# Decode attention and SwiGLU on one core: the negation of the row maximum moved from GpSimd to ScalarE, a fourth V buffer, and a feed-forward computed transposed

## The chip, the core and the metric

The kernel runs on one core of a Trainium2 chip. A core has five engines with an instruction stream each: TensorE (PE in the profile; PEld are its weight loads), VectorE (DVE), ScalarE (ACT), GpSimd (POOL) and SyncE (SP), which here only starts transfers. They meet at semaphores. Sixteen DMA engines move data from the memory of the chip (HBM) to the on-chip memory of 128 partitions (SBUF); TensorE writes to PSUM. The metric is the time of one execution in microseconds on the device, the median of several.

## The reference

One decode step for a batch of 4: layer norm, attention over a cache of 4096 positions with 32 heads of width 192, a residual, layer norm, a SwiGLU feed-forward, a residual. All inputs are bf16.

```python
q = (layernorm(x) @ wq)                    # 4 x 640 @ 640 x 6144 -> 4 x 32 heads x 192
scores = einsum("bhqd,bhkd->bhqk", q, k_cache) * 192 ** -0.5     # k_cache 4 x 32 x 4096 x 192
o = einsum("bhqk,bhkd->bhqd", softmax(scores), v_cache)
h = x + o.reshape(4, 1, 6144) @ wo
n = layernorm(h)
out = h + (silu(n @ w_gate) * (n @ w_up)) @ w_down               # w_gate, w_up 640 x 1536
```

There is no reuse: each of the 128 pairs of head and batch row (called heads below, n = 4 x head + row) has its own K and V of 1.57 MB each.

## The kernel before, in words

**A head.** K of one head lies on 128 partitions with 32 rows of 192 each (`kbuf`, 4 buffers), V likewise (`vbuf`, `NB_V` = 3 buffers). Its query is spread over all partitions by a small TensorE product (`qbmm`, L679) and copied by ScalarE (`qbcopy`, L518, into `qb`). VectorE forms the 4096 scores in 32 multiply-and-sum instructions (L422), which write one column of `S` each, and takes the maximum per partition (L431, `pmax`). GpSimd takes the maximum over partitions (L336, `gmax`) and negates it (L339, `negmax`). ScalarE computes exp(S + negmax) into `E` with the sum per partition (L585, `rowsum`). GpSimd sums over partitions (L343, `gsum`). VectorE takes the reciprocal (L437) and scales `E` (L447). TensorE then adds up the head's output in 32 products (`pv`, L694). GpSimd's loop has these three operations in this order for each head and nothing else.

**Heads by TensorE.** Every eighth head, n = 5, 13, ... 117 (15 of them, `p_heads`), gets its scores from TensorE instead: `pwork` transposes K in eight slabs of 8 transposes (L737, L739), ScalarE copies each slab out of PSUM (`pcopies`, L542 and L543), and TensorE multiplies it with the query in 8 one-column products (L751, L753). ScalarE copies the scores to `S` (L556). Such a head takes its place in the softmax four heads later (the list `order`; the rank of a head is its place there).

**The order of the work** is written out by hand for each engine. VectorE's step s does the scores of head s, the maximum of rank s-1, the reciprocal of rank s-2 and the scaling of rank s-3. ScalarE's step s does the exponential of rank s, then the slab copies of head s+1 if that is a p head, then the query copy of head s+4, then copies of outputs. TensorE's step s does the query products of head s+4 (and of head s+5 where the step has a `pwork`), `pwork` of head s+2 if that is a p head, and `pv` of rank s-2; the output projection of a pair of heads comes a few steps later (`ott`, `womm`). SyncE issues the loads in one order: K of head m as soon as head m-4 is used up (for a p head: transposed), then V of rank m-5 as soon as `pv` of NB_V ranks earlier is done. A load that has to wait holds up those behind it.

**Ends.** Ahead of the loop stands a layer norm (with 1/sqrt as exp(-0.5 ln), L561 and L564). After it come the residual (L452), the second layer norm (L621, L624), the transposes of its result into `hlnT` (L815), and the feed-forward in three chunks of 512 columns: five gate and five up products of 512 columns each with `hlnT` as weights (L824, L827), then three copies out of PSUM by ScalarE (L633 sigmoid, L635, L637), before the next chunk. VectorE multiplies the three results (L472, L475), TensorE transposes the product in 12 pieces (L834), ScalarE copies it (L642), and the down product follows (L839, L841).

Of the kernel before, what the change touches and what calls it, by code (L numbers as in the profile page):

```python
# [5 lines left out]
ACT = mybir.ActivationFunctionType  # L6
ALU = mybir.AluOpType
AX = mybir.AxisListType
ReduceOp = bass.bass_isa.ReduceOp
BF16 = mybir.dt.bfloat16  # L10
# [15 lines left out]
def bass_sequential_preLN__gqa_block_cached__swiglu_ffn__decode_kernel(  # L26
# [12 lines left out]
    B, _sq, D = A_x.shape  # L39
# [3 lines left out]
    F = B_w_gate.shape[1]  # L43
# [5 lines left out]
    KT = D // 128  # L49
    FT = F // 128  # L50
    NQBLK = QD // 512
    NFC = F // 512
# [3 lines left out]
    PAIRK = (2 * DH) // 128  # L56
    assert PAIRK * 128 == 2 * DH
    WOK = QD // 128
    NB_K, NB_V, NQB, NS, NP = 4, 3, 4, 4, 4
    NE = 2 * B  # L60
    QLA = 4
    att_scale = float(DH) ** -0.5
# [3 lines left out]
    def hb(n):  # L66
        return n // B, n % B
# [3 lines left out]
    NPH = len(p_heads)  # L71
# [10 lines left out]
    NSLAB = JQ // SLAB_T  # L82
# [29 lines left out]
    for k in range(NH):  # L112
        n = order[k]
        s = e4slot(n)
# [58 lines left out]
    stp = [pe_step_chunk[j] for j in sorted(pe_step_chunk)]  # L173
    assert all(stp[i + 1] > stp[i] + 3 for i in range(len(stp) - 1)), stp

    DV_VEPS1, DV_XLN = 4, 5
    DV_H, DV_VEPS2, DV_HLN, DV_GU, DV_FINAL = 6, 9, 10, 12, 13
    AC_RSTD1, AC_XLNT = 2, 3
    AC_RSTD2, AC_HLNT = 5, 6
    AC_GUC = [6 + 3 * (c + 1) for c in range(NFC)]  # L180
    AC_GU = AC_GUC[-1]
    AC_GUT = AC_GU + 1
    PE_XT = 1
    PE_HT = 2
    PE_FFN1 = [2 + (c + 1) for c in range(NFC)]
    PE_GUT = PE_FFN1[-1] + 1
    PE_DOWN = PE_GUT + 1
    PL_READY = 2 + NE

    es = ExitStack()  # L190
    with es:  # L191
        E_ = es.enter_context
# [4 lines left out]
        rstd1 = E_(nc.sbuf_tensor("rstd1", [B, 1], FP32))  # L197
# [13 lines left out]
        gmax = E_(nc.sbuf_tensor("gmax", [128, NP], FP32))  # L211
        negmax = E_(nc.sbuf_tensor("negmax", [128, NP], FP32))
# [8 lines left out]
        wg_sb = E_(nc.sbuf_tensor("wg_sb", [128, KT, F], BF16))  # L221
        wu_sb = E_(nc.sbuf_tensor("wu_sb", [128, KT, F], BF16))
# [4 lines left out]
        rstd2 = E_(nc.sbuf_tensor("rstd2", [B, 1], FP32))  # L227
        hln_bf = E_(nc.sbuf_tensor("hln_bf", [B, D], BF16))
        hlnT = E_(nc.sbuf_tensor("hlnT", [128, KT, B], BF16))
        sig_sb = E_(nc.sbuf_tensor("sig_sb", [B, F], BF16))  # L230
        g_sb = E_(nc.sbuf_tensor("g_sb", [B, F], BF16))
        u_sb = E_(nc.sbuf_tensor("u_sb", [B, F], BF16))
        gu_sb = E_(nc.sbuf_tensor("gu_sb", [B, F], BF16))
        guT = E_(nc.sbuf_tensor("guT", [128, FT, B], BF16))
        out_bf = E_(nc.sbuf_tensor("out_bf", [B, D], BF16))
        psqb = [E_(nc.psum_tensor(f"psqb{i}", [128, 512], FP32)) for i in range(2)]
# [5 lines left out]
        psT32 = psT.bitcast(FP32)  # L242
        psM16 = psM.bitcast(BF16)
        PSS_COL0 = 0
        QCOL_A = DH
        QCOL_B = DH + 1
        OTC0 = 512
# [70 lines left out]
        @block.gpsimd  # L318
        def _(eng):
            eng.memset(ident[:, :], 0.0)  # L320
            i1 = eng.memset(sel[:, :, :], 0.0)
            c_pl.inc(i1)
            for s in range(NE):
                i1 = eng.memset(E4[s][:, :, :], 0.0)
                c_pl.inc(i1)
            eng.wait_ge(c_pl.sem, 1)
            eng.affine_select(out=ident[:, :], in_=ident[:, :], compare_op=ALU.not_equal,
                              fill=1.0, base=0, pattern=[[-1, 128]], channel_multiplier=1)
            i1 = eng.affine_select(out=sel[:, :, :], in_=sel[:, :, :], compare_op=ALU.not_equal,
                                   fill=1.0, base=0, pattern=[[-1, B], [0, 128]], channel_multiplier=1)  # L330
            pl_ready = c_pl.inc(i1)
            assert pl_ready == PL_READY
            for k in range(NH):
                s = k % NP
                eng.wait_ge(c_rm.sem, k + 1)
                i1 = eng.partition_all_reduce(gmax[:, s:s + 1], pmax[:, s:s + 1], 128, ReduceOp.max)  # L336
                c_ar.inc(i1)
                eng.wait_ge(c_ar.sem, k + 1)
                i1 = eng.tensor_scalar(out=negmax[:, s:s + 1], in0=gmax[:, s:s + 1],  # L339
                                       scalar1=-1.0, scalar2=None, op0=ALU.mult)  # L340
                c_neg.inc(i1)
                eng.wait_ge(c_exp.sem, k + 1)
                i1 = eng.partition_all_reduce(gsum[:, s:s + 1], rowsum[:, s:s + 1], 128, ReduceOp.add)  # L343
                c_tot.inc(i1)
# [43 lines left out]
        def _(eng):  # L388
# [11 lines left out]
            i1 = eng.tensor_scalar(out=rstd1[:, :], in0=mv1[:, 1:2], scalar1=1e-5, scalar2=None, op0=ALU.add)  # L400
            v = c_dv.inc(i1)
            assert v == DV_VEPS1
            eng.wait_ge(c_ac.sem, AC_RSTD1)
            i1 = eng.tensor_scalar(out=xln_bf[:, :], in0=x_f[:, :], scalar1=mv1[:, 0:1], scalar2=rstd1[:, 0:1],
                                   op0=ALU.subtract, op1=ALU.mult)
            v = c_dv.inc(i1)
# [56 lines left out]
            i1 = eng.tensor_scalar(out=rstd2[:, :], in0=mv2[:, 1:2], scalar1=1e-5, scalar2=None, op0=ALU.add)  # L463
            v = c_dv.inc(i1)
            assert v == DV_VEPS2
            eng.wait_ge(c_ac.sem, AC_RSTD2)
            i1 = eng.tensor_scalar(out=hln_bf[:, :], in0=h_f[:, :], scalar1=mv2[:, 0:1], scalar2=rstd2[:, 0:1],
                                   op0=ALU.subtract, op1=ALU.mult)
            v = c_dv.inc(i1)
            assert v == DV_HLN  # L470
            eng.wait_ge(c_ac.sem, AC_GU)
            i1 = eng.tensor_tensor(out=gu_sb[:, :], in0=g_sb[:, :], in1=sig_sb[:, :], op=ALU.mult)  # L472
            v = c_dv.inc(i1)
            eng.wait_ge(c_dv.sem, v)
            i1 = eng.tensor_tensor(out=gu_sb[:, :], in0=gu_sb[:, :], in1=u_sb[:, :], op=ALU.mult)  # L475
            v = c_dv.inc(i1)
            assert v == DV_GU
            eng.wait_ge(c_pe.sem, PE_DOWN)
# [5 lines left out]
        def _(eng):  # L484
# [73 lines left out]
                assert v2 == pi + 1  # L558

            eng.wait_ge(c_dv.sem, DV_VEPS1)  # L560
            i1 = eng.activation(out=rstd1[:, :], in_=rstd1[:, :], func=ACT.Ln)  # L561
            v = c_ac.inc(i1)
            eng.wait_ge(c_ac.sem, v)
            i1 = eng.activation(out=rstd1[:, :], in_=rstd1[:, :], func=ACT.Exp, scale=-0.5)  # L564
            v = c_ac.inc(i1)
            assert v == AC_RSTD1
            eng.wait_ge(c_pe.sem, PE_XT)
            i1 = eng.activation(out=xlnT[:, :, :], in_=psT[:, 0:KT * B], func=ACT.Copy)
            v = c_ac.inc(i1)
# [6 lines left out]
            for s in range(NH + 8):  # L576
                k = s
                if k < NH:
                    m = order[k]
                    hm, bm = hb(m)  # L580
                    eng.wait_ge(c_neg.sem, k + 1)
                    prv = prev_same_slot[m]
                    if prv is not None:
                        eng.wait_ge(c_pv.sem, rank[prv] + 1)
                    i1 = eng.activation(out=E4[e4slot(m)][:, :, bm], in_=S[k % NS][:, :], func=ACT.Exp,  # L585
                                        bias=negmax[:, (k % NP):(k % NP) + 1], scale=1.0,
                                        accum_out=rowsum[:, (k % NP):(k % NP) + 1])
                    v2 = c_exp.inc(i1)
                    assert v2 == k + 1
# [28 lines left out]
            assert c_oc.n == NGRP and c_otc.n == NPAIR and c_qbc.n == NH and c_exp.n == NH and c_qc.n == NQBLK  # L618
            assert c_kc.n == NPH * NSLAB and c_pS.n == NPH
            eng.wait_ge(c_dv.sem, DV_VEPS2)  # L620
            i1 = eng.activation(out=rstd2[:, :], in_=rstd2[:, :], func=ACT.Ln)  # L621
            v = c_ac.inc(i1)
            eng.wait_ge(c_ac.sem, v)
            i1 = eng.activation(out=rstd2[:, :], in_=rstd2[:, :], func=ACT.Exp, scale=-0.5)  # L624
            v = c_ac.inc(i1)
            assert v == AC_RSTD2
            eng.wait_ge(c_pe.sem, PE_HT)
            i1 = eng.activation(out=hlnT[:, :, :], in_=psT[:, 0:KT * B], func=ACT.Copy)
            v = c_ac.inc(i1)
            assert v == AC_HLNT  # L630
            for c in range(NFC):
                eng.wait_ge(c_pe.sem, PE_FFN1[c])
                i1 = eng.activation(out=sig_sb[:, c * 512:(c + 1) * 512], in_=psqb[0][0:B, 0:512], func=ACT.Sigmoid)  # L633
                c_ac.inc(i1)
                i1 = eng.activation(out=g_sb[:, c * 512:(c + 1) * 512], in_=psqb[0][0:B, 0:512], func=ACT.Copy)  # L635
                c_ac.inc(i1)
                i1 = eng.activation(out=u_sb[:, c * 512:(c + 1) * 512], in_=psqb[1][0:B, 0:512], func=ACT.Copy)  # L637
                v = c_ac.inc(i1)
                assert v == AC_GUC[c]
            assert v == AC_GU  # L640
            eng.wait_ge(c_pe.sem, PE_GUT)
            i1 = eng.activation(out=guT[:, :, :], in_=psT[:, 0:FT * B], func=ACT.Copy)  # L642
            v = c_ac.inc(i1)
            assert v == AC_GUT

        @block.tensor
        def _(eng):
# [169 lines left out]
            assert v == PE_HT  # L817
            eng.wait_ge(c_ac.sem, AC_HLNT)
            eng.wait_ge(sem_ffn, 48)
            for c in range(NFC):  # L820
                if c >= 1:
                    eng.wait_ge(c_ac.sem, AC_GUC[c - 1])
                for k in range(KT):
                    eng.matmul(psqb[0][0:B, 0:512], lhsT=hlnT[:, k, :], rhs=wg_sb[:, k, c * 512:(c + 1) * 512],  # L824
                               start=(k == 0), stop=(k == KT - 1))
                for k in range(KT):
                    i1 = eng.matmul(psqb[1][0:B, 0:512], lhsT=hlnT[:, k, :], rhs=wu_sb[:, k, c * 512:(c + 1) * 512],  # L827
                                    start=(k == 0), stop=(k == KT - 1))
                v = c_pe.inc(i1)
                assert v == PE_FFN1[c]  # L830
            eng.wait_ge(c_dv.sem, DV_GU)
            eng.wait_ge(c_ac.sem, AC_GU)
            for k in range(FT):
                i1 = eng.transpose(out=psT[:, k * B:(k + 1) * B], in_=gu_sb[0:B, k:F:FT], identity=identB)  # L834
            v = c_pe.inc(i1)
            assert v == PE_GUT
            eng.wait_ge(c_ac.sem, AC_GUT)
            for k in range(FT):
                eng.matmul(acc[0:B, 0:512], lhsT=guT[:, k, :], rhs=wd_sb[:, k, 0:512],  # L839
                           start=(k == 0), stop=(k == FT - 1))  # L840
# [34 lines left out]
```

## Time and profile before

| | |
|---|---|
| median of 6 executions | 2244.94 us (2239.03 to 2255.18) |
| profiled execution | span 2237.2 us, 23426 instructions |
| busy: PE, PEld, DVE, ACT, POOL | 935.1, 667.7, 1080.1, 235.3, 136.8 us |
| moved by DMA | 425.80 MB, mean 190 GB/s |
| mean granted TensorE clock | 0.619 |

A row of the groups gives line, engine, operation, output and inputs, the number of instructions, the busy time in us, the mean of one in ns, and after the bar the idle time of the engine just ahead of them with what ended most of it. "issue" stands where the trace shows nothing that the engine waited for. Engine names with a q (POOLq) are the sequencer of that engine. In the timeline a row gives start, length, engine, line, operation, and in brackets the idle time ahead of it.

### The profile page before, as it was taken

To read this page: it belongs to the slowest core of one execution; us is meant where nothing else is said; L and a number is where in the kernel's file an instruction comes from. 1 tells how busy PE (TensorE), PEld (TensorE's weight loads), DVE (VectorE), ACT (ScalarE), POOL (GpSimd) and SP (SyncE) were. 2 spreads that over 40 slices of the span, in tenths; PEclk is the share of its full clock that TensorE was granted. 3 is DMA by queue.
4 is the path that set the end of the run, shared out by engine and by line. 5 is a ranking of instruction groups with operands and counts; after the bars stand their busy time and mean duration, and the time that the engine had idled before them with its cause. 6 is when DMAs were issued, how large, how long until landed. Compare 5 with 4: busy or idle time off the path is not lost.

```text
span 2237.2 us, 23426 instructions
## 1 busy us (share of the span) xinstructions
PE 935.1 (42%) x6439; PEld 667.7 (30%) x6439; DVE 1080.1 (48%) x7631; ACT 235.3 (11%) x735; POOL 136.8 (6%) x400
## 2 busy tenths in 40 slices
PE   1162532635326262352634425453262634426235
PEld 0141321424214242241422314332141422314222
DVE  5465444555535555444554536555354554545551
ACT  1010100201001010110101002010010101001001
POOL 0000000000000000000000000000000000000000
PEclk7565565665656666566655656656565665656667
DMA  7354383542737436274361745527374361736430
GB/s 288 122 214 185 117 342 122 242 188 109 293 148 281 171 120 272 101 317 173 154 246 68 305 176 209 225 74 292 122 281 182 153 250 71 310 144 249 183 113 1
DMA packets 44339, 425.80 MB, mean 190 GB/s; under 512 B 4520, under 2 KB 5808, under 8 KB 11056
## 3 DMA queue, kind: packets, MB, share of 16 engines
q1 hardware_dynamic: 38192, 404.65, 45.8%
q10 hardware_dynamic: 6016, 19.66, 2.5%
q8 instruction: 51, 0.84, 0.1%
q14 instruction: 80, 0.66, 0.1%
HBM read 424.29 MB, written 0.01 MB: 190 GB/s over the span
## 4 chain that ended last, share of the span: by engine, by line
issue 77%; PE 13%; POOL 5%; ACT 3%; DVE 1%; POOLq 1%; ACTq 0%; DVEq 0%
PE psqb L739 4%; PE psqb L737 4%; POOL gsum L343 2%; PE psT L751 2%; PE psT L753 2%; POOL gmax L336 2%; POOL negmax L339 1%; ACT E L585 1%; DVE kbuf L422 1%; ACT kt L543 1%; ACT kt L542 0%; PE psO L694 0%; POOLq L339 0%; POOLq L191 0%; PE psqb L824 0%
## 5 line engine op out<-in xcount | busy, mean ns | idle before, releaser
L422 DVE CUSTOM_DVE_ANT_0 kbuf<-kbuf,qb 128x192 bf16<-128x192 bf16 x3616 | 1019.2, 353 | 13.5 <-ACT qb L518 13.3
L694 PE MATMUL psO<-vbuf,E 128*4 128x192 bf16 x4096 | 518.6, 307 | 387.7 <-DVE E L447 371.1
L694 PEld LDWEIGHTS psO<-vbuf,E 128*4 128x4 bf16 x4096 | 422.6, 106 | 470.3 <-DVE E L447 380.6
L437 DVE RECIPROCAL rtot<-gsum 128x1 f32<-128x1 f32 x128 | 21.0, 164 | 1101.3 <-POOL gsum L343 1101.3
L422 DVE DVE_READ_ACCUMULATOR2_ANT S<- 128x1 f32 x3616 | 295.6, 82 | 0.0
L679 PE MATMUL psM<-QO_sb,sel 4*128 4x192 bf16 x113 | 32.7, 290 | 626.8 <-ACT qb L518 319.2
L585 ACT ACTIVATE E<-S,negmax 128x32 bf16<-128x32 f32 x128 | 46.7, 365 | 1627.9 <-POOL negmax L339 1627.8
L679 PEld LDWEIGHTS psM<-QO_sb,sel 4*128 4x128 bf16 x113 | 10.7, 95 | 651.5 <-issue 414.6
L751 PE MATMUL psT<-qcolA,kt 128*128 128x1 bf16 x480 | 88.6, 185 | 183.9 <-ACT kt L543 183.9
L739 PE MATMUL psqb<-ident,kbuf 128*64 128x128 bf16 x480 | 151.7, 316 | 0.0
L737 PE MATMUL psqb<-ident,kbuf 128*128 128x128 bf16 x480 | 138.1, 288 | 0.0
L343 POOL PARTITION_ALL_REDUCE gsum<-rowsum x128 | 51.3, 401 | 981.6 <-issue 888.8
L751 PEld LDWEIGHTS psT<-qcolA,kt 128*128 128x128 bf16 x480 | 49.6, 103 | 203.1 <-issue 171.2
L339 POOL TENSOR_SCALAR negmax<-gmax 128x1 f32<-128x1 f32 x128 | 36.6, 286 | 1044.5 <-issue 1044.5
L542 ACT ACTIVATE kt<-psqb 128x512 bf16<-128x512 bf16 x120 | 71.1, 592 | 160.6 <-PE psqb L739 160.6
L753 PE MATMUL psT<-qcolB,kt 64*128 64x1 bf16 x480 | 87.8, 183 | 0.0
L739 PEld LDWEIGHTS psqb<-ident,kbuf 128*64 128x64 bf16 x480 | 61.4, 128 | 56.1
L543 ACT ACTIVATE kt<-psqb 64x512 bf16<-64x512 bf16 x120 | 69.4, 579 | 0.0
L737 PEld LDWEIGHTS psqb<-ident,kbuf 128*128 128x128 bf16 x480 | 49.8, 104 | 48.1 <-issue 2.7
L336 POOL PARTITION_ALL_REDUCE gmax<-pmax x128 | 56.3, 440 | 22.7 <-DVE pmax L431 22.7
L518 ACT ACTIVATE qb<-psM 128x192 bf16<-128x192 f32 x113 | 36.2, 320 | 157.0 <-PE psM L679 157.0
L753 PEld LDWEIGHTS psT<-qcolB,kt 64*128 64x128 bf16 x480 | 48.9, 102 | 7.0
(74 smaller groups left out, 232.9 us busy)
## 6 DMA issues: line engine op xcount, KB each, us to landing
kbuf<-in_A_k_cache_dram SPq DMA_DIRECT2D x128, 1536.0 KB, 8.6
vbuf<-in_A_v_cache_dram SPq DMA_DIRECT2D x128, 1536.0 KB, 10.1
wo_sb<-in_A_wo_dram ACTq DMA_DIRECT2D x16, 480.0 KB, 3.5
wq_sb<-in_A_wq_dram ACTq DMA_DIRECT2D x4, 1280.0 KB, 5.9
wg_sb<-in_B_w_gate_dram ACTq DMA_DIRECT2D x1, 1920.0 KB, 13.1
wu_sb<-in_B_w_up_dram ACTq DMA_DIRECT2D x1, 1920.0 KB, 13.4
wd_sb<-in_B_w_down_dram ACTq DMA_DIRECT2D x1, 1920.0 KB, 14.1
wq_sb<-in_A_wq_dram SPq DMA_DIRECT2D x1, 1280.0 KB, 5.8
```

Source lines behind the costliest of these rows:

```text
L336: i1 = eng.partition_all_reduce(gmax[:, s:s + 1], pmax[:, s:s + 1], 128, ReduceOp.max)
L339: i1 = eng.tensor_scalar(out=negmax[:, s:s + 1], in0=gmax[:, s:s + 1], scalar1=-1.0, scalar2=None, op0=ALU.mult)
L343: i1 = eng.partition_all_reduce(gsum[:, s:s + 1], rowsum[:, s:s + 1], 128, ReduceOp.add)
L422: i1 = eng.tensor_tensor_reduce(out=sl, in0=sl, in1=qb[qs][:, :], scale=1.0, scalar=0.0, op0=ALU.mult, op1=ALU.add, accum_out=S[ss][:, j:j ...
L542: eng.activation(out=kt1[g % 2][:, :], in_=psb16[g % 2][:, 0:SW], func=ACT.Copy)
L543: i1 = eng.activation(out=kt2[g % 2][:, :], in_=psb16[g % 2][0:64, SW:2 * SW], func=ACT.Copy)
L585: i1 = eng.activation(out=E4[e4slot(m)][:, :, bm], in_=S[k % NS][:, :], func=ACT.Exp, bias=negmax[:, (k % NP):(k % NP) + 1], scale=1.0, ac ...
L694: i1 = eng.matmul(psO[h % 2][0:B, 0:DH], lhsT=E4[e4slot(m)][:, j, :], rhs=vbuf[k % NB_V][:, j * DH:(j + 1) * DH], start=(first and j == 0) ...
L737: eng.transpose(out=psb16[g % 2][:, i * 128:(i + 1) * 128], in_=kbuf[sk][:, j * DH:j * DH + 128], identity=ident[:, :])
L739: i1 = eng.transpose(out=psb16[g % 2][0:64, SW + i * 128:SW + (i + 1) * 128], in_=kbuf[sk][:, j * DH + 128:j * DH + DH], identity=ident[:, :])
L751: eng.matmul(psT32[:, PSS_COL0 + j:PSS_COL0 + j + 1], lhsT=kt1[g % 2][:, i * 128:(i + 1) * 128], rhs=qcolA[qs][:, 0:1], start=True, stop=F ...
L753: i1 = eng.matmul(psT32[:, PSS_COL0 + j:PSS_COL0 + j + 1], lhsT=kt2[g % 2][0:64, i * 128:(i + 1) * 128], rhs=qcolB[qs][0:64, 0:1], start=F ...
```

## The change

It has four parts. The negation of the maximum goes from GpSimd to ScalarE, directly ahead of the exponential that uses it. V gets a fourth buffer. Both layer norms use Sqrt on ScalarE and a reciprocal on VectorE instead of Ln and Exp on ScalarE. The feed-forward is computed transposed: slices of the gate and up weights (128 columns, every twelfth) are TensorE's stationary operand and `hlnT` (4 columns) is the moving one, 60 products for gate and 60 for up, so that the results stand as 128 x 48 in PSUM and need no copies and no transposes ahead of the down product. The aim is less work on GpSimd and ScalarE's PSUM copies, more slack for V, and a shorter end.

```diff
-    NB_K, NB_V, NQB, NS, NP = 4, 3, 4, 4, 4
+    NB_K, NB_V, NQB, NS, NP = 4, 4, 4, 4, 4
...
# GpSimd, in the loop over heads
                 i1 = eng.partition_all_reduce(gmax[:, s:s + 1], pmax[:, s:s + 1], 128, ReduceOp.max)
                 c_ar.inc(i1)
-                eng.wait_ge(c_ar.sem, k + 1)
-                i1 = eng.tensor_scalar(out=negmax[:, s:s + 1], in0=gmax[:, s:s + 1],
-                                       scalar1=-1.0, scalar2=None, op0=ALU.mult)
-                c_neg.inc(i1)
                 eng.wait_ge(c_exp.sem, k + 1)
...
# ScalarE, in the loop over steps
+                    eng.wait_ge(c_ar.sem, k + 1)
+                    i1 = eng.activation(out=negmax[:, (k % NP):(k % NP) + 1], in_=gmax[:, (k % NP):(k % NP) + 1],
+                                        func=ACT.Copy, scale=-1.0)
+                    c_neg.inc(i1)
                     eng.wait_ge(c_neg.sem, k + 1)
...
# layer norms (the second likewise): ScalarE, then VectorE
-            i1 = eng.activation(out=rstd1[:, :], in_=rstd1[:, :], func=ACT.Ln)
...
-            i1 = eng.activation(out=rstd1[:, :], in_=rstd1[:, :], func=ACT.Exp, scale=-0.5)
+            i1 = eng.activation(out=rstd1[:, :], in_=rstd1[:, :], func=ACT.Sqrt)
...
+            i1 = eng.reciprocal(rstd1[:, :], rstd1[:, :])
...
# feed-forward, TensorE (up likewise into psU)
-                for k in range(KT):
-                    eng.matmul(psqb[0][0:B, 0:512], lhsT=hlnT[:, k, :], rhs=wg_sb[:, k, c * 512:(c + 1) * 512],
-                               start=(k == 0), stop=(k == KT - 1))
+            for t in range(FT):
                 for k in range(KT):
+                    i1 = eng.matmul(psG[:, t * B:(t + 1) * B], lhsT=wg_sb[:, k, t:F:FT], rhs=hlnT[:, k, :],
+                                    start=(k == 0), stop=(k == KT - 1))
...
-                i1 = eng.transpose(out=psT[:, k * B:(k + 1) * B], in_=gu_sb[0:B, k:F:FT], identity=identB)
...
# feed-forward, ScalarE and VectorE
-                i1 = eng.activation(out=sig_sb[:, c * 512:(c + 1) * 512], in_=psqb[0][0:B, 0:512], func=ACT.Sigmoid)
-                i1 = eng.activation(out=g_sb[:, c * 512:(c + 1) * 512], in_=psqb[0][0:B, 0:512], func=ACT.Copy)
-                i1 = eng.activation(out=u_sb[:, c * 512:(c + 1) * 512], in_=psqb[1][0:B, 0:512], func=ACT.Copy)
+            i1 = eng.activation(out=sigT[:, :], in_=psG, func=ACT.Sigmoid)
...
+            i1 = eng.tensor_tensor(out=gsT[:, :], in0=psG, in1=sigT[:, :], op=ALU.mult)
...
+            i1 = eng.tensor_tensor(out=guT[:, :, :], in0=gsT[:, :], in1=psU, op=ALU.mult)
```

More of the change, by code (lines that the diff above doesn't have):

```diff
@@ L174, in bass_sequential_preLN__gqa_block_cached__swiglu_ffn__decode_kernel @@
     assert all(stp[i + 1] > stp[i] + 3 for i in range(len(stp) - 1)), stp
[L176 to L187, printed above, removed]
+    DV_VEPS1, DV_RSTD1, DV_XLN = 4, 5, 6
+    DV_H, DV_VEPS2, DV_RSTD2, DV_HLN, DV_GU, DV_FINAL = 7, 10, 11, 12, 14, 15
+    AC_SQRT1, AC_XLNT = 1, 2
+    AC_SQRT2, AC_HLNT, AC_SIG = 3, 4, 5
+    PE_XT, PE_HT, PE_FFN_G, PE_FFN_U, PE_DOWN = 1, 2, 3, 4, 5
     PL_READY = 2 + NE
@@ L229, in bass_sequential_preLN__gqa_block_cached__swiglu_ffn__decode_kernel @@
         hlnT = E_(nc.sbuf_tensor("hlnT", [128, KT, B], BF16))
[L230 to L233, printed above, removed]
+        sigT = E_(nc.sbuf_tensor("sigT", [128, FT * B], BF16))
+        gsT = E_(nc.sbuf_tensor("gsT", [128, FT * B], BF16))
         guT = E_(nc.sbuf_tensor("guT", [128, FT, B], BF16))
@@ L244, in bass_sequential_preLN__gqa_block_cached__swiglu_ffn__decode_kernel @@
         PSS_COL0 = 0
+        psG = psqb[0][:, 0:FT * B]
+        psU = psqb[1][:, 0:FT * B]
         QCOL_A = DH
@@ L402, in _ @@
             assert v == DV_VEPS1
-            eng.wait_ge(c_ac.sem, AC_RSTD1)
+            eng.wait_ge(c_ac.sem, AC_SQRT1)
+            i1 = eng.reciprocal(rstd1[:, :], rstd1[:, :])
+            v = c_dv.inc(i1)
+            assert v == DV_RSTD1
+            eng.wait_ge(c_dv.sem, v)
             i1 = eng.tensor_scalar(out=xln_bf[:, :], in0=x_f[:, :], scalar1=mv1[:, 0:1], scalar2=rstd1[:, 0:1],
@@ L465, in _ @@
             assert v == DV_VEPS2
-            eng.wait_ge(c_ac.sem, AC_RSTD2)
+            eng.wait_ge(c_ac.sem, AC_SQRT2)
+            i1 = eng.reciprocal(rstd2[:, :], rstd2[:, :])
+            v = c_dv.inc(i1)
+            assert v == DV_RSTD2
+            eng.wait_ge(c_dv.sem, v)
             i1 = eng.tensor_scalar(out=hln_bf[:, :], in0=h_f[:, :], scalar1=mv2[:, 0:1], scalar2=rstd2[:, 0:1],
@@ L470, in _ @@
             assert v == DV_HLN
-            eng.wait_ge(c_ac.sem, AC_GU)
-            i1 = eng.tensor_tensor(out=gu_sb[:, :], in0=g_sb[:, :], in1=sig_sb[:, :], op=ALU.mult)
+            eng.wait_ge(c_ac.sem, AC_SIG)
+            i1 = eng.tensor_tensor(out=gsT[:, :], in0=psG, in1=sigT[:, :], op=ALU.mult)
             v = c_dv.inc(i1)
             eng.wait_ge(c_dv.sem, v)
-            i1 = eng.tensor_tensor(out=gu_sb[:, :], in0=gu_sb[:, :], in1=u_sb[:, :], op=ALU.mult)
+            eng.wait_ge(c_pe.sem, PE_FFN_U)
+            i1 = eng.tensor_tensor(out=guT[:, :, :], in0=gsT[:, :], in1=psU, op=ALU.mult)
             v = c_dv.inc(i1)
@@ L560, in _ @@
             eng.wait_ge(c_dv.sem, DV_VEPS1)
-            i1 = eng.activation(out=rstd1[:, :], in_=rstd1[:, :], func=ACT.Ln)
+            i1 = eng.activation(out=rstd1[:, :], in_=rstd1[:, :], func=ACT.Sqrt)
             v = c_ac.inc(i1)
-            eng.wait_ge(c_ac.sem, v)
-            i1 = eng.activation(out=rstd1[:, :], in_=rstd1[:, :], func=ACT.Exp, scale=-0.5)
-            v = c_ac.inc(i1)
-            assert v == AC_RSTD1
+            assert v == AC_SQRT1
             eng.wait_ge(c_pe.sem, PE_XT)
@@ L620, in _ @@
             eng.wait_ge(c_dv.sem, DV_VEPS2)
-            i1 = eng.activation(out=rstd2[:, :], in_=rstd2[:, :], func=ACT.Ln)
+            i1 = eng.activation(out=rstd2[:, :], in_=rstd2[:, :], func=ACT.Sqrt)
             v = c_ac.inc(i1)
[L623 to L626, printed above, removed]
+            assert v == AC_SQRT2
             eng.wait_ge(c_pe.sem, PE_HT)
@@ L630, in _ @@
             assert v == AC_HLNT
-            for c in range(NFC):
-                eng.wait_ge(c_pe.sem, PE_FFN1[c])
-                i1 = eng.activation(out=sig_sb[:, c * 512:(c + 1) * 512], in_=psqb[0][0:B, 0:512], func=ACT.Sigmoid)
-                c_ac.inc(i1)
-                i1 = eng.activation(out=g_sb[:, c * 512:(c + 1) * 512], in_=psqb[0][0:B, 0:512], func=ACT.Copy)
-                c_ac.inc(i1)
-                i1 = eng.activation(out=u_sb[:, c * 512:(c + 1) * 512], in_=psqb[1][0:B, 0:512], func=ACT.Copy)
[L638 to L642, printed above, removed]
+            eng.wait_ge(c_pe.sem, PE_FFN_G)
+            i1 = eng.activation(out=sigT[:, :], in_=psG, func=ACT.Sigmoid)
             v = c_ac.inc(i1)
-            assert v == AC_GUT
+            assert v == AC_SIG
         @block.tensor
@@ L819, in _ @@
             eng.wait_ge(sem_ffn, 48)
-            for c in range(NFC):
-                if c >= 1:
-                    eng.wait_ge(c_ac.sem, AC_GUC[c - 1])
+            if NPH > 0:
+                eng.wait_ge(c_kc.sem, NPH * NSLAB)
+            eng.wait_ge(c_qc.sem, NQBLK)
+            for t in range(FT):
                 for k in range(KT):
-                    eng.matmul(psqb[0][0:B, 0:512], lhsT=hlnT[:, k, :], rhs=wg_sb[:, k, c * 512:(c + 1) * 512],
-                               start=(k == 0), stop=(k == KT - 1))
+                    i1 = eng.matmul(psG[:, t * B:(t + 1) * B], lhsT=wg_sb[:, k, t:F:FT], rhs=hlnT[:, k, :],
+                                    start=(k == 0), stop=(k == KT - 1))
+            v = c_pe.inc(i1)
+            assert v == PE_FFN_G
+            for t in range(FT):
                 for k in range(KT):
-                    i1 = eng.matmul(psqb[1][0:B, 0:512], lhsT=hlnT[:, k, :], rhs=wu_sb[:, k, c * 512:(c + 1) * 512],
+                    i1 = eng.matmul(psU[:, t * B:(t + 1) * B], lhsT=wu_sb[:, k, t:F:FT], rhs=hlnT[:, k, :],
                                     start=(k == 0), stop=(k == KT - 1))
-                v = c_pe.inc(i1)
-                assert v == PE_FFN1[c]
+            v = c_pe.inc(i1)
+            assert v == PE_FFN_U
             eng.wait_ge(c_dv.sem, DV_GU)
-            eng.wait_ge(c_ac.sem, AC_GU)
-            for k in range(FT):
-                i1 = eng.transpose(out=psT[:, k * B:(k + 1) * B], in_=gu_sb[0:B, k:F:FT], identity=identB)
-            v = c_pe.inc(i1)
-            assert v == PE_GUT
-            eng.wait_ge(c_ac.sem, AC_GUT)
             for k in range(FT):
```

## The prediction

> **What bounds the kernel now.** I read the page's engine shares first (DVE 48%, PE 42%, DMA about half: nothing full), then its chain (77% "issue": an engine held by nothing the trace names), then the groups, to see which engine that is.
>
> ```profile
> L422 DVE CUSTOM_DVE_ANT_0 kbuf<-kbuf,qb 128x192 bf16<-128x192 bf16 x3616 | 1019.2, 353 | 13.5 <-ACT qb L518 13.3
> ...
> L343 POOL PARTITION_ALL_REDUCE gsum<-rowsum x128 | 51.3, 401 | 981.6 <-issue 888.8
> ...
> L339 POOL TENSOR_SCALAR negmax<-gmax 128x1 f32<-128x1 f32 x128 | 36.6, 286 | 1044.5 <-issue 1044.5
> ...
> L336 POOL PARTITION_ALL_REDUCE gmax<-pmax x128 | 56.3, 440 | 22.7 <-DVE pmax L431 22.7
> ```
>
> After the bar stands the idle time before a group. GpSimd is busy 137 us, yet idle 1044.5 us before its negation and 981.6 us before its sum: 2026 us of 2237. The order in time for GpSimd (start, length, line, idle before):
>
> ```profile
> 1002.43 0.40 POOL L343 PARTITION_ALL_REDUCE gsum<-rowsum  x1 [13.35 <-issue]
> 1002.75 0.44 POOL L336 PARTITION_ALL_REDUCE gmax<-pmax  x1
> 1010.53 0.31 POOL L339 TENSOR_SCALAR negmax<-gmax 128x1 f32<-128x1 f32 x1 [7.34 <-issue]
> 1016.67 0.40 POOL L343 PARTITION_ALL_REDUCE gsum<-rowsum  x1 [5.83 <-issue]
> 1016.99 0.44 POOL L336 PARTITION_ALL_REDUCE gmax<-pmax  x1
> ```
>
> Two all-reduces in a row start 0.32 us apart, so an all-reduce is short. Only going from one to the negation (7.34 us idle) and back (5.83 us) is long. The view by source line says why:
>
> ```profile
> L339 POOLq MODIFY_POOL_CONFIG  x256: 82/83/83, 38.4 to 2184.6; - x128
> ...
> L336 POOLq MODIFY_POOL_CONFIG  x2: 1/1/1, 15.5 to 15.6; - x2
> ...
> L343 POOLq MODIFY_POOL_CONFIG  x256: 5/7/7, 50.8 to 2191.9; - x128
> ```
>
> Each negation, and each sum after it, reconfigures GpSimd; the maximum after a sum does not, but for one pair at the start. So one head costs two reconfigurations in series with the exponential between them: (1044.5 + 981.6)/128 = 15.8 us of its 2237/128 = 17.5 us. That is the bound.
>
> [...]
>
> **The change, part by part.**
>
> *Negation to ScalarE (L339 gone).* Removes 128 negations and both reconfigurations of each head. Adds 128 one-column copies on ScalarE; the like copy L512 takes 0.15 us, and with the wait on its own semaphore I take 0.25 (0.15 to 0.4), 32 us in all on an engine 11% busy. The wait for the maximum now stands at ScalarE's head, but the exponential behind it waited there already (1627.8 us, for negmax), so nothing new queues behind it. The head's chain max, all-reduce, negate, exp, all-reduce becomes 0.44 + 0.25 + 0.56 + 0.40 us and hand-offs, about 2 us instead of 17.
>
> So the next bound has to be found. VectorE's own work:
>
> ```profile
> 1067.98 0.30 DVE L447 TENSOR_SCALAR E<-E,rtot 128x32 bf16<-128x32 bf16 x1
> 1077.20 0.19 DVE L431 TENSOR_REDUCE pmax<-S 128x1 f32<-128x32 f32 x1
> 1082.18 0.16 DVE L437 RECIPROCAL rtot<-gsum 128x1 f32<-128x1 f32 x1 [4.79 <-POOL gsum L343]
> ```
>
> Scale to maximum is 9.2 us: 32 products (0.279 us apart, 8.94 us) and the issue gap. With maximum, reciprocal and scale a head is 9.4 us. The 15 heads p (5, 13, ... 117) that go by TensorE cost VectorE 0.45. Floor of eight heads: 7 x 9.4 + 0.45 = 66.3 us. Transfers of eight heads: 16 loads of 1.573 MB and 1.2 MB of weights, 26.4 MB. Rate when the queues are full, and PE in a p head (columns: window, then busy time of PE, PEld, DVE, ACT, POOL, clock, DMA share, GB/s):
>
> ```profile
> 1084.00:1088.00 4.00, 4.00 (x22) 2.36 (x22) 4.00 (x29) 1.24 (x3) 0.00 (x0) 0.50 0.00 0
> ...
> 1116.00:1120.00 4.00, 0.00 (x0) 0.00 (x0) 3.20 (x23) 0.00 (x0) 0.76 (x2) 0.50 1.02 436
> 1120.00:1124.00 4.00, 0.00 (x0) 0.00 (x0) 4.00 (x29) 0.00 (x0) 0.00 (x0) 0.50 1.00 415
> 1124.00:1128.00 4.00, 0.31 (x2) 0.14 (x3) 2.26 (x17) 0.48 (x3) 0.26 (x1) 0.50 1.01 423
> ```
>
> At 420 GB/s that is 63 us. So VectorE is the floor, DMA close below, and what VectorE waits for in eight heads adds to it. I walk one period by hand, from t = 0 at the end of the product of head p-1:
> - p has no VectorE product, so the reciprocal of p-2 comes at once and waits for its chain, begun at 0.2: ready at about 2.2. Products of p+1 run from 2.65 to 11.6, of p+2 from 12.05 to 21.0.
> - TensorE's work on p can begin when ScalarE has copied the query of p+2, behind the exponential of p-2: about 2.3. Eight slabs of 8 transposes (1.87 us a slab, 1078.33 to 1080.20) and 8 products (0.94 us): 22.5 us, end at about 25.
> - ScalarE copies these slabs in order and reaches the next exponential only behind the last, at about 24.5. Its sum is there at 25.6, where VectorE has waited from 21.1; it goes on at 26.1.
> - Five steps of 9.4 less the last 0.45 end at 72.6. All later queries are copied in time (the next, p+4, at about 33 behind two head sums of 7.1 us together; needed at 35.5).
> - Transfers: the K load of p+4 waits for the last transpose (about 23) and blocks the queue; 63 us from there end at 88, that is 15 into the next period, before its 23. So DMA has 8 us to spare.
>
> Period 72.6 us: 66.3 and two waits (2.2 and about 4.1).
>
> *Fourth V buffer.* A V load then waits for the head sum four heads back, not three. Within the walk it lets V of p-1 and K of p+5 go at 23 rather than after the first head sum at about 30; both are needed after 32, K at 45. Hidden beside VectorE: 0, or up to 2 us a period if loads land late.
>
> *Tail.* Before, from h (2208.04) to the end 29.2 us. Sqrt and a VectorE reciprocal for Ln and Exp: 2210.20 to 2211.95 becomes about 0.5 us; one exposed table load of 1.28 goes, Sqrt's stays hidden as Ln's was: -1.3. FFN: 30 wide products, 9 copies, 2 wide multiplies, 12 transposes and a copy (2213.2 to 2229.55, 16.4 us) become 120 weight loads with 4-column products. The nearest row, L751 with L753, runs load and product at 0.117 us: 14.0 us. From below 0.065 us (the 12 transposes L834, weights of the same stride 12, take 0.78 us) gives 8; from above, twice, if 128 strided partitions load slower, 28. I take 14, plus 0.5 for the last multiply: -1.8. The sigmoid, its table load and its multiply lie under the up products. Tail 26.1 (20 to 40).
>
> *Sqrt at the start*: hidden, TensorE waits there for GpSimd's sel until 15.5.
>
> **The sum.** First product at 19.8 as before; five heads end at 65.5. 15 periods: 1089, to 1154.5. The last three heads: 28.2, 1182.7. Last chain to the scale of head 125: 2.65, its head sum cold 5.3, two more at 2.8, output product 2.5: 13.3 + 2.8 for starts and hand-offs, to 1198.8. Tail 26.1: span 1225. The six times lie about 2 to 8 us above spans; I say 1230.
>
> **Rivals.**
> - *A. ScalarE behind the slabs does not hold VectorE, or TensorE's slabs run quicker*: only the 2.2 us waits stay, 68.5 us a period, 1168. For it: VectorE is the fullest engine. Against: no slab in the trace runs off clock 0.50.
> - *B. A new wait dominates*: the K load behind the last transpose, or V loads, starve VectorE[...]. Period 77 to 85: 1295 to 1415. For it: the sync queue already waits 722.4 us for L739. Against: windows at 400 GB/s and more, 8 us spare.
> - *C. The all-reduce itself is slow*, some 7 us, its record showing only a part; the negation is innocent. Then GpSimd stays the bound and ScalarE adds a hand-off: 128 x 0.1 us more, 2255, slower. [...] Against: 0.32 us between two all-reduces.
>
> **How the numbers follow.** Forecast 0.62, A 0.14, B 0.21, C 0.03. Range 1165 to 1345: the forecast and its tail bounds, most of A, the nearer half of B. Below it lies only the bare VectorE floor (about 1135), above it the far half of B and C. Faster 0.97, same 0.01, slower 0.02 (C mostly, its small remainder is no change).
>
> **What would show it.** Right: two MODIFY_POOL_CONFIG pairs in place of some 256; gmax and gsum with no "issue" idle of 6 us; VectorE about 88% busy in every slice; its largest waits at L437, once in eight heads some 4 us. Wrong: spacing of all-reduces still 6 us (C); idle before L422 on K loads (B); the FFN products at over 0.2 us each (tail).

## The result

The changed kernel takes 1200.71 us (median of 8, 1200.26 to 1202.07) against 2251.73 us for the kernel before (median of 16; the 2244.94 us further up is of the first six): a ratio of 0.5336, 95% interval 0.5325 to 0.5347. The forecast was 1230 us with a range of 1165 to 1345.

The groups of the profile after, with the same columns as before. GpSimd's lines are now L329 (maximum) and L332 (sum), the products L415, the negation L577:

```profile
L415 DVE CUSTOM_DVE_ANT_0 kbuf<-kbuf,qb 128x192 bf16<-128x192 bf16 x3616 | 1017.9, 352 | 16.5 <-ACT qb L516 14.8
...
L577 ACT ACTIVATE negmax<-gmax 128x1 f32<-128x1 f32 x128 | 25.5, 199 | 481.3 <-POOL gmax L329 481.2
L329 POOL PARTITION_ALL_REDUCE gmax<-pmax x128 | 63.7, 497 | 627.1 <-DVE pmax L424 627.0
...
L430 DVE RECIPROCAL rtot<-gsum 128x1 f32<-128x1 f32 x128 | 20.0, 156 | 84.6 <-POOL gsum L332 84.5
L332 POOL PARTITION_ALL_REDUCE gsum<-rowsum x128 | 51.9, 406 | 412.9 <-ACT E L584 412.9
```

GpSimd's idle time is still over 1000 us, but its releasers have names now: it waits for VectorE and ScalarE (627.0 and 412.9 us), where most of it stood under "issue" before. VectorE's wait for the sum fell to 84.5 us; in the kernel before it was 1101.3:

```profile
L437 DVE RECIPROCAL rtot<-gsum 128x1 f32<-128x1 f32 x128 | 21.0, 164 | 1101.3 <-POOL gsum L343 1101.3
```

The products cost what they did (1019.2 us, now 1017.9) and fill 85% of the span instead of 46%. Two lines of the page, the busy shares of VectorE and of the DMA engines in 40 slices:

```profile
DVE  4989989999998989989898998989989898998981
...
DMA  6759979897999969989896997969799796997960
```

Of the pairs of MODIFY_POOL_CONFIG, the view by source line shows one on the lines of the loop, where each of two lines had 128. A second pair stands in the set-up ahead of it, at L320.

```profile
L329 POOLq MODIFY_POOL_CONFIG  x2: 1/1/1, 15.6 to 15.6; - x2
```

Such a pair, with the idle time of GpSimd that follows it, is called a reconfiguration from here on.

The timeline of VectorE over one p head (563.10 is the end of the product of head p-1; the products themselves are left out):

```profile
563.10 0.18 DVE L424 TENSOR_REDUCE pmax<-S 128x1 f32<-128x32 f32 x1
...
564.91 0.16 DVE L430 RECIPROCAL rtot<-gsum 128x1 f32<-128x1 f32 x1 [1.33 <-POOL gsum L332]
...
574.32 0.15 DVE L430 RECIPROCAL rtot<-gsum 128x1 f32<-128x1 f32 x1
...
583.57 0.19 DVE L424 TENSOR_REDUCE pmax<-S 128x1 f32<-128x32 f32 x1
588.08 0.16 DVE L430 RECIPROCAL rtot<-gsum 128x1 f32<-128x1 f32 x1 [4.32 <-POOL gsum L332]
```

One wait of 1.33 us where the p head has no product of its own, one of 4.32 us two steps later. The next p head's long wait ends at 659.54: a period of 71.5 us.

### The profile page after: what moved, and what is told of

Read it like the earlier page. It is cut to its first block, busy times and chain, and to the rows that moved or that the text cites. A ratio compares the mean times of both kernels' runs of the same rounds, so it can differ in the third digit from the quotient of the medians.

```text
span 1200.6 us, 23061 instructions
## 1 busy us (share of the span) xinstructions
PE 891.0 (74%) x6517; PEld 651.7 (54%) x6517; DVE 1065.9 (89%) x7633; ACT 258.2 (22%) x851; POOL 115.0 (10%) x272
## 4 chain that ended last, share of the span: by engine, by line
DVE 51%; PE 37%; DMA 4%; issue 4%; ACT 2%; POOL 1%; ACTq 0%; SPq 0%; DVEq 0%; POOLq 0%
DVE kbuf L415 47%; PE psqb L725 10%; PE psqb L723 9%; PE psO L680 9%; DMA vbuf<-in_A_v_cache_dram 4%; PE psT L737 4%; PE psT L739 4%; DVE S L415 2%; DVE E L440 1%; ACT kt L541 1%; PE psM L665 1%; POOL gsum L332 0%; ACT qb L516 0%; DVE pmax L424 0%; PE acc L823 0%
## 5 line engine op out<-in xcount | busy, mean ns | idle before, releaser
L415 DVE CUSTOM_DVE_ANT_0 kbuf<-kbuf,qb 128x192 bf16<-128x192 bf16 x3616 | 1017.9, 352 | 16.5 <-ACT qb L516 14.8
L680 PE MATMUL psO<-vbuf,E 128*4 128x192 bf16 x4096 | 483.5, 294 | 193.3 <-DMA vbuf<-in_A_v_cache_dram 144.2
L680 PEld LDWEIGHTS psO<-vbuf,E 128*4 128x4 bf16 x4096 | 403.0, 101 | 256.3 <-issue 158.3
L415 DVE DVE_READ_ACCUMULATOR2_ANT S<- 128x1 f32 x3616 | 292.6, 81 | 0.0
L577 ACT ACTIVATE negmax<-gmax 128x1 f32<-128x1 f32 x128 | 25.5, 199 | 481.3 <-POOL gmax L329 481.2
L329 POOL PARTITION_ALL_REDUCE gmax<-pmax x128 | 63.7, 497 | 627.1 <-DVE pmax L424 627.0
L430 DVE RECIPROCAL rtot<-gsum 128x1 f32<-128x1 f32 x128 | 20.0, 156 | 84.6 <-POOL gsum L332 84.5
L332 POOL PARTITION_ALL_REDUCE gsum<-rowsum x128 | 51.9, 406 | 412.9 <-ACT E L584 412.9
```

Source lines behind the costliest of these rows:

```text
L415: i1 = eng.tensor_tensor_reduce(out=sl, in0=sl, in1=qb[qs][:, :], scale=1.0, scalar=0.0, op0=ALU.mult, op1=ALU.add, accum_out=S[ss][:, j:j ...
L680: i1 = eng.matmul(psO[h % 2][0:B, 0:DH], lhsT=E4[e4slot(m)][:, j, :], rhs=vbuf[k % NB_V][:, j * DH:(j + 1) * DH], start=(first and j == 0) ...
```

## The experiments

**1. Each part alone.** The negation alone on the kernel before, then with the fourth V buffer, whose diff against the kernel before is

```diff
-                eng.wait_ge(c_ar.sem, k + 1)
-                i1 = eng.tensor_scalar(out=negmax[:, s:s + 1], in0=gmax[:, s:s + 1],
-                                       scalar1=-1.0, scalar2=None, op0=ALU.mult)
-                c_neg.inc(i1)
...
+                    eng.wait_ge(c_ar.sem, k + 1)
+                    i1 = eng.activation(out=negmax[:, (k % NP):(k % NP) + 1], in_=gmax[:, (k % NP):(k % NP) + 1],
+                                        func=ACT.Copy, scale=-1.0)
+                    c_neg.inc(i1)
```

and for the second besides `NB_V` 3 to 4.

> The kernel before with the negation moved to ScalarE and nothing else (three V buffers, the old layer norms and feed-forward). If the two reconfigurations of GpSimd per head were the bound: the time of the changed kernel plus its shorter tail, 29.2 - 20.4 = 8.8 us, so about 1210 us, and up to 1225 if three V buffers make VectorE wait. If buffer or feed-forward carry a share of their own in the new regime: above 1250.

> The kernel before with the negation moved and four V buffers, old layer norms and feed-forward. Theory (the fourth buffer is hidden beside VectorE): equal to the run with the negation alone within 0.5%, about 1209 us. Rival (late V loads reach VectorE): 15 to 30 us below that run.

Measured: 1214.09 us (ratio 0.5395, 0.5377 to 0.5413) and 1211.31 us (0.5385, 0.5368 to 0.5402). The negation alone brings nearly everything. The two differ by less than their intervals, so the fourth buffer's worth here is not told from nothing; the third step, to the changed kernel's 0.5336, is the tail's.

The reverse, the changed kernel with the negation back on GpSimd:

> The changed kernel with the negation back on GpSimd. Theory: the old bound returns whole, two reconfigurations per head, and only the shorter tail stays: before minus 9 us, a ratio of about 0.996. Rival (buffer and tail matter): below 0.98.

Measured: 2280.46 us, a ratio of 1.0139 (1.0102 to 1.0176). The old bound returned, but 1.4% slower than before where 0.4% faster was expected. So something in the rest costs time under the old bound. The buffer and the tail (the layer norms and the feed-forward, which no run separates) were each tried alone on the kernel before:

> The kernel before with four V buffers and nothing else. The run with the negation back on GpSimd came out 1.4% slower than before where 0.4% faster was expected. Theory: [...] (in the trace of before 7.1 us to the negation at a DMA share under 0.1, 11.1 us at one over 0.9); then this kernel is slower than before, a ratio of 1.01 to 1.025. Rival (something in the new tail or the layer norms did it): 1.00 within 0.3%.

> The kernel before with the new layer norms and feed-forward and nothing else. Theory (the buffer made the loss): 9 us less than before, a ratio of 0.996. Rival (the tail made it): above 1.005.

Measured: 2289.54 us, 1.0212 (1.0156 to 1.0269), with the buffer alone; 2230.73 us, 0.9951 (0.9927 to 0.9975), with the tail alone. The buffer made the loss. The group of the negation with the fourth buffer alone, whose idle time was 1044.5 us before:

```profile
L339 POOL TENSOR_SCALAR negmax<-gmax 128x1 f32<-128x1 f32 x128 | 36.1, 282 | 1106.4 <-issue 1106.4
```

What a V buffer may have to do with a wait of GpSimd is seen in windows of the kernel before, laid over four idle stretches of GpSimd in a row, from the end of one operation to the start of the next (the last three columns are TensorE's clock, the DMA share and GB/s). The first and third end at a negation, the second and fourth at a sum:

```profile
1003.19:1010.53 7.34, 7.06 (x42) 4.61 (x42) 7.34 (x54) 0.00 (x0) 0.00 (x1) 0.69 0.07 28
1010.84:1016.67 5.83, 0.28 (x2) 0.19 (x2) 1.40 (x11) 0.72 (x4) 0.00 (x1) 0.81 0.61 209
1017.43:1026.20 8.77, 5.43 (x38) 4.08 (x38) 8.77 (x64) 0.00 (x0) 0.00 (x1) 0.78 0.45 188
1026.47:1036.44 9.97, 0.24 (x1) 0.09 (x1) 0.01 (x1) 0.53 (x4) 0.00 (x1) 0.58 0.83 316
```

With such a window for every negation (those from 60 us on, of before and of the fourth buffer alone), sorted by the DMA share in it, worked out from the two traces:

| DMA share in the stretch | before: count, mean idle | fourth buffer: count, mean idle |
|---|---|---|
| under 0.1 | 54, 7.10 us | 63, 7.08 us |
| 0.1 to 0.7 | 53, 8.34 us | 36, 8.87 us |
| 0.7 and more | 20, 10.35 us | 28, 11.76 us |

The stretches beside full transfers are 3.3 us (before) to 4.7 us (fourth buffer) longer than those with almost none. In all, the idle time ahead of the negations grew by 62 us and the kernel's time by 48, so the loss lies in these stretches. Why they grew is less plain. That 28 of them instead of 20 fall beside transfers at 0.7 and more doesn't account for it: with the means of before, the counts of the fourth buffer give 5 us. Taken rank by rank, 52 of the 62 us fall on one rank in eight (6, 14, and so on, counted from 0). Its stretch took 8.0 us before, at a mean share of 0.64, and takes 11.3 us with the buffer, at 0.94. That V, requested earlier, fills this stretch fits both numbers. It is still a comparison of stretches that differ in more than the transfers, and no run moved the transfers alone; by what path transfers would lengthen a reconfiguration is not shown.

**2. Is it the negation's place or its kind?** Behind the sum, the changed kernel was given an instruction of the same kind whose result nobody reads, and in a second kernel one of another kind instead. `scrap` and `scrap2` are new tiles of one column each.

```diff
                 i1 = eng.partition_all_reduce(gsum[:, s:s + 1], rowsum[:, s:s + 1], 128, ReduceOp.add)
                 c_tot.inc(i1)
+                eng.tensor_scalar(out=scrap[:, :], in0=scrap2[:, :], scalar1=-1.0, scalar2=None, op0=ALU.mult)
# the second kernel, instead:
+                eng.memset(scrap[:, :], 0.0)
```

> The changed kernel with an added GpSimd tensor_scalar per head, behind the sum, that writes one column nobody reads. No value waits for it. Theory [...]: about 15 us per head in series again, 2050 to 2300 us, and some 256 reconfigurations on each of two lines. Rival (the negation cost by standing in the chain from maximum to exponential): 1200 to 1215 us.

> The changed kernel with an added GpSimd memset of one column per head, behind the sum, that nobody reads. Theory ([...]the memsets at the start run with no reconfiguration ahead of them): within 5 us of the changed kernel, about 1201 us, and two reconfigurations. Rival (a third instruction of any kind in GpSimd's loop costs some microseconds): above 1300 us.

Measured: 2399.06 us and 1200.04 us, one execution each. The groups of the first:

```profile
L332 POOL PARTITION_ALL_REDUCE gmax<-pmax x128 | 48.4, 378 | 946.7 <-issue 922.5
L337 POOL TENSOR_SCALAR scrap<-scrap 128x1 f32<-128x1 f32 x128 | 37.0, 289 | 1115.8 <-issue 1115.8
...
L335 POOL PARTITION_ALL_REDUCE gsum<-rowsum x128 | 50.3, 393 | 174.2 <-ACT E L588 174.2
```

its MODIFY_POOL_CONFIG pairs, and below them those of the second kernel:

```profile
L332 POOLq MODIFY_POOL_CONFIG  x256: 1/7/8, 3.7 to 2361.0; - x128
L337 POOLq MODIFY_POOL_CONFIG  x256: 83/83/83, 30.7 to 2368.3; - x128
```

```profile
L332 POOLq MODIFY_POOL_CONFIG  x2: 1/1/1, 15.8 to 15.8; - x2
```

and the timeline of GpSimd in the second:

```profile
1015.21 0.38 POOL L335 PARTITION_ALL_REDUCE gsum<-rowsum  x1 [12.47 <-ACT E L588]
1015.46 0.16 POOL L337 MEMSET scrap<- 128x1 f32 x1
1015.52 0.42 POOL L332 PARTITION_ALL_REDUCE gmax<-pmax  x1
```

An instruction that nobody waits for doubles the time, if it makes GpSimd reconfigure; around a memset two all-reduces start 0.31 us apart. The range expected for the first was missed by 99 us on the high side. Against the kernel before, the rows show the added time in two places. There the exponential ran during GpSimd's reconfiguration for the sum, and 15 of 128 sums waited for it (92.8 us); here the reconfiguration stands elsewhere, and all 128 sums wait for the exponential in full view (174.2 us). And the reconfigurations took 105 us more in all (1115.8 and 922.5 us under "issue" against 1044.5 and 888.8); why is not shown.

**3. VectorE's two waits.** ScalarE's slab copies of a p head were split, so that the exponential of rank p does not stand behind all eight:

```diff
                     if p_act_step[p] == s:
-                        pcopies(p)
+                        pcopies(p, 0, 4)
+                    if p_act_step[p] + 1 == s:
+                        pcopies(p, 4, 8)
```

> The changed kernel with ScalarE's eight slab copies of a p head split: four, then the next exponential (rank p), then four. If VectorE's wait of 4.3 us once per eight heads comes from that exponential standing behind all slabs, this wait at the reciprocal of rank p goes. But the next exponential (rank p+1) still follows the query copy of p+4, which TensorE feeds only after two head sums at about 33 us into the period; VectorE would reach its reciprocal at about 30 instead of 34.5, so the wait returns there, some 4 us: 1185 to 1205 us, a wait moved and not removed. Rival (the wait is simply that exponential): 4.3 x 15 = 65 us less, about 1137 us.

Measured: 1198.87 us (0.5333, 0.5308 to 0.5359), no change that can be told. The reciprocals of one period:

```profile
562.02 0.16 DVE L430 RECIPROCAL rtot<-gsum 128x1 f32<-128x1 f32 x1 [1.34 <-POOL gsum L332]
571.43 0.15 DVE L430 RECIPROCAL rtot<-gsum 128x1 f32<-128x1 f32 x1
580.80 0.15 DVE L430 RECIPROCAL rtot<-gsum 128x1 f32<-128x1 f32 x1
594.87 0.16 DVE L430 RECIPROCAL rtot<-gsum 128x1 f32<-128x1 f32 x1 [4.64 <-POOL gsum L332]
```

The wait left the third reciprocal and stands, as long, at the fourth: moved, not removed. What holds it now is in ScalarE's timeline. A query copy waits for its product on TensorE, which stands there behind two head sums (64 products, 585.18 to 593.07), and the next exponential stands behind this copy:

```profile
593.29 0.33 ACT L516 ACTIVATE qb<-psM 128x192 bf16<-128x192 f32 x1 [9.10 <-PE psM L670]
...
593.95 0.36 ACT L569 ACTIVATE E<-S,negmax 128x32 bf16<-128x32 f32 x1
```

The next kernel takes this holder away and, in the same edit, one that might follow: the exponential of rank p+1 behind the last slab. Against the last diff:

```diff
                     if p_act_step[p] + 1 == s:
-                        pcopies(p, 4, 8)
+                        pcopies(p, 4, 7)
+                        expstep(s + 1)      # negation and exponential of rank p+1
+                        pcopies(p, 7, 8)
# in its own step, expstep of that rank is left out
...
# TensorE
                     if p_pe_step[p] == s:
                         pwork(p)
+                        if p + 4 < NH and (p + 4) not in qb_emitted:
+                            qbmm(p + 4)
+                            qb_emitted.add(p + 4)
```

> As the split run, and besides: the exponential of rank p+1 ahead of the last slab copy, and TensorE's query product of head p+4 directly behind the slabs, ahead of the head sums. If exponentials and query copies behind the slabs are all that VectorE waits for: up to 65 us less than the changed kernel, about 1140 us. What may hold it: K of p+4 is requested at 22.6 us into the period and needed at about 30, so a load of over 7.5 us gives back up to 3 us a period (1140 to 1185 us); and the transfers fill 62 us of a period that would be 67. If DMA is the bound already: no gain, 1195 us and more.

Measured: 1147.15 us (0.5110, 0.5092 to 0.5129), 54 us less than the changed kernel. VectorE's waits of this kernel (us in total, times, longest):

```profile
DVE rtot L430 <- POOL gsum L332: 22.5, 17, 1.3
DVE kbuf L415 <- ACT qb L516: 14.4, 1, 14.4
DVE kbuf L415 <- DMA kbuf<-in_A_k_cache_dram: 13.3, 8, 3.6
```

The long wait is gone and the short one remains. The waits for the sum fell from 84.5 us to 22.5, by 62; of these, 11.8 come back as waits for K loads (13.3 us against 1.5 in the changed kernel). Only 1.2 us of the 13.3, at two heads p+4, are for the K load behind the last transpose, which the expectation named; the rest stands at other heads. The transfers have little room left: from 66 to 1100 us the DMA share is 0.93, against 0.89 in the changed kernel. So a wait in a schedule written out by hand had two holders in a row, and taking away the first alone showed nothing. Whether the exponential behind the last slab would have been a third is not told, since no run takes away the second holder alone.

**4. The feed-forward products** took half of what was forecast. Does the stride of 12 columns cost anything?

```diff
-                    i1 = eng.matmul(psG[:, t * B:(t + 1) * B], lhsT=wg_sb[:, k, t:F:FT], rhs=hlnT[:, k, :],
+                    i1 = eng.matmul(psG[:, t * B:(t + 1) * B], lhsT=wg_sb[:, k, t * 128:(t + 1) * 128], rhs=hlnT[:, k, :],
                                     start=(k == 0), stop=(k == KT - 1))
# up likewise; the rows of the down weights laid out to match
-        wd_view = B_w_down.rearrange("(p k) c -> p k c", k=FT)
+        wd_view = B_w_down.rearrange("(k p) c -> p k c", k=FT)
```

> The changed kernel with the gate and up weights taken as 128 adjacent columns instead of every twelfth, and the rows of the down weights laid out to match. It asks why the 120 products took 0.061 us each where 0.117 was forecast. If weights of stride 12 load slower than adjacent ones: below 0.055 us each. If stride is free: 0.061 us each and no change of the time.

Measured: 1195.13 us, one execution. The groups of the gate products, of the changed kernel and of this one:

```profile
L811 PE MATMUL psqb<-hlnT,wg_sb 128*128 128x4 bf16 x60 | 3.8, 200 | 0.3 <-ACT hlnT L624 0.3
```

```profile
L811 PE MATMUL psqb<-hlnT,wg_sb 128*128 128x4 bf16 x60 | 1.8, 167 | 0.3 <-ACT hlnT L624 0.3
```

Busy 3.8 us for 60 becomes 1.8, at a clock of 0.50 in both: weights of stride 12 cost twice the time of adjacent ones. The gate and up products together give 4.0 of the 5.6 us by which the whole time fell.

**5. Both gains together.**

> The split run with both exponentials moved, and the gate and up weights as adjacent columns. The two gains lie at different places of the path and should add: 1147 less 4 us of products and up to 2 us more, 1140 to 1144 us. If the end of the kernel were held by something else than these products: 1147 us.

Measured: 1143.69 us (1142.06 to 1144.29), a ratio of 0.5102 (0.5088 to 0.5116): 57 us under the changed kernel, and the fastest of all.

## Why the prediction was right

**The bound.** The step that carried it, that the time around the negation is GpSimd's reconfiguration and not the all-reduce, the negation or its wait, holds: the tensor_scalar that nobody reads brings it back, the memset does not, two all-reduces start 0.31 us apart with a memset between, and moving the negation alone gives a ratio of 0.5395. Rival C is excluded by this. One reconfiguration is not as long as another: the lines that the prediction shows have 5.83, 7.34 and 13.35 us of idle time.

**The new bound.** VectorE is busy 89% of the span (about 88% was named as the sign). The walk through one period gave waits of 2.2 and about 4.1 us; the trace has 1.33 and 4.32. It had the second end at t = 26.1; it ended at 588.08 - 563.10 = 25.0. The cause it gave, ScalarE behind the slabs, is shown by the splits, with the refinement that a second holder stands behind it. It put the end of DMA's work 8 us before the next K request (63 us from its 23 end at 86 and not 88, so nearly 10 by its own figures). In the trace this holds for some periods and not for others. The windows, with the columns as before, are ahead of three requests, at 371.71, 585.74 and 657.21:

```profile
368.00:372.00 4.00, 4.00 (x24) 2.46 (x23) 3.44 (x25) 1.36 (x3) 0.00 (x0) 0.50 0.63 264
...
580.00:584.00 4.00, 4.00 (x27) 2.68 (x26) 3.72 (x27) 2.12 (x4) 0.00 (x0) 0.50 0.24 101
...
648.00:652.00 4.00, 4.00 (x25) 2.54 (x24) 4.00 (x31) 1.46 (x3) 0.00 (x0) 0.50 0.09 37
652.00:656.00 4.00, 4.00 (x25) 2.54 (x24) 3.31 (x25) 1.76 (x4) 0.00 (x0) 0.50 0.00 0
```

It was enough: VectorE waited 1.5 us in all for K, so rival B did not come. Rival A did not either. All slabs of 13 of the 15 p heads ran at clock 0.50. In two, one of them the head shown above, the first two or three slabs ran at a clock of 0.82 to 1.00 (1.40 to 1.54 us for the transposes of one instead of 1.93), and the rest at 0.50.

**Not foreseen:** V does arrive late for TensorE (46 waits, 144.2 us in all, against 1.1 us before). None of VectorE's waits is put down to a V load, but the chain of work that ended last passes through V loads for 4% of the span, so that they cost nothing is not shown.

**The sizes.** The span was put at 1225 and is 1200.6. By terms:

| term | forecast | measured |
|---|---|---|
| end of the last product | 1182.7 | 1163.9 |
| last chain, to the residual | 16.1 | 16.3 |
| tail | 26.1 | 20.4 |
| allowance from span to time | 5 | 1.8 |

The sum of the measured terms, 1202.4, is the time of the profiled execution; the median of the other eight is 1200.71.

The first term was mis-sized in the period: it is 71.4 us on average (1064.52 less 65.10, over 14 periods) where 72.6 was forecast, and 15 times the difference is 18 of the 18.8 us. The larger part is VectorE's waits: from its first to its last product they come to 83.7 us, where 15 times 6.3, or 94.5, was forecast, above all because the short wait is 1.33 us and not 2.2. The rest, 8 us, is the step of VectorE: 9.4 us a head was taken from a sum of parts, and the commonest distance of two maxima is 9.23.

The last chain agrees by luck. The prediction started the last cold head sum 2.65 us behind the last product and counted 2.8 us once for "two more at 2.8"; in the trace the cold one starts after 0.5 us (5.28 us long, at clock 0.50) and three more follow it (96 products in 8.22 us, at 0.98).

The tail was mis-sized by the price of a product: 0.117 us was taken from the rows of the score products, and the 120 products took 7.3 us, 0.061 each, below the 0.065 that stood as the lower bound. The layer norm gave the 1.3 us that were forecast. The nearest row by operation was not the nearest by cost. Why the score products take twice as long stays open. The down products ran at a mean clock of 0.55 and took 6.15 us, against 5.13 us at 0.67 before.

**The fourth buffer** was costed at nothing to 2 us a period; the two runs with and without it differ by 2.8 us in all, which can't be told from nothing. That it costs 2.1% under the old bound the prediction did not ask, and did not need.

## What to carry to other kernels

When an engine stands idle under "issue" between short operations, compare neighbours of the same kind with neighbours of different kinds: 0.3 us against 6 to 13 us was the whole finding, and one tensor_scalar of 0.29 us a head on GpSimd was worth half of the time (2399.06 us with it, 1200.71 without). When such a bound falls, walk one period of the next one by hand with durations from the trace: which engine is full, what the next instruction of its stream waits for, and what stands behind that; a wait may have more than one holder, and taking away the first alone may show nothing. The buffer that could not be told from nothing under the new bound (2.8 us less) cost 2.1% under the old one.

## What the runs showed of the hardware that was not expected

- GpSimd's reconfiguration for the negation was longer beside transfers, though no run moved the transfers alone: the stretch ahead of a negation took 7.1 us at a DMA share under 0.1 and 10.4 (before) to 11.8 us (fourth buffer) at 0.7 and more. Under the old bound a fourth V buffer alone made the kernel 2.1% slower, and the time went into these stretches.
- Stationary operands of 128 x 128 with columns 12 elements apart: 0.061 us a load and product with 4 moving columns, against 0.028 us with adjacent columns (120 in 7.3 us and in 3.3 us, both at clock 0.50).
- A memset between all-reduces brought no reconfiguration on GpSimd (one pair in the loop's lines), where a tensor_scalar brought 128 pairs on each of two lines.
- Transposes with one-column products between them kept TensorE busy for some 20 us at a time, at a clock of 0.50 in all slabs of 13 of 15 p heads; in the other two the first two or three slabs ran at 0.82 to 1.00 and the rest at 0.50.
